# Gated linear attention and spectral filter on one core: token stage in 64-row parts, reversed key blocks, and products that may be issued in column tiles

## The chip, the cores and the metric

The kernel runs on one core of one Trainium2 chip. The metric is the device time of one launch in microseconds (us). Three runs of the kernel before the change took 241.71, 242.41 and 244.06 us, so its median is 242.41 us. Besides, one execution was profiled; durations and shares below are from that execution. The engines are named as in the profile: PE is the matrix engine (PEld its weight loads), DVE the vector engine, ACT the scalar engine, POOL the GpSimd engine, and SP the engine whose queue issues nearly all DMAs.

## The reference

The input x has 2048 tokens of 640 channels in bf16. Two branches read it, and a gate per token mixes them.

```python
x = A_x                                              # (1, 2048, 640)
g = sigmoid((x * gate_w).sum(-1, keepdims=True))
a = A(x)      # 32 heads of 20: per segment of 512 tokens causal softmax attention,
              # mixed with a read of a linear memory M, z that earlier segments filled
b = irfft2(rfft2(x) * (w_r + 1j * w_i))              # over tokens and channels
return g * a + (1 - g) * b
# inside A, for each of 4 segments s:
#   a_dot = softmax(q k^T / sqrt(20) + causal mask) v
#   a_mem = (phi(q) M) / (phi(q) z + 1e-6);  o = sig(beta) a_mem + (1 - sig(beta)) a_dot
#   M += phi(k)^T v;  z += sum phi(k)                ; finally o @ wo
```

## The kernel before, in words

**Attention branch.** For each segment s of 512 tokens, `project` makes q and k (products of 128 weight columns with 512 or twice 256 moving columns, `proj`, 195 operations), stores them to a scratch tensor and loads them back padded per head (`pad`). v is made per block of 128 tokens in two halves of 320 or 321 columns (`vproj`, 160 operations). The keys of the odd 128-token blocks stand in an order in which the two halves of 64 tokens are exchanged (`token_order`), and the v products of the odd blocks are issued as two tiles of 64 columns each so that their rows stand in that order too. `qk_unit` makes the logits of four heads in row tiles (80 units), ACT takes the exponential out of PSUM (92 instructions, line 1265), POOL zeroes what the causal mask forbids (`mask`, line 1286, 224 instructions), and `pv_flipped` (segments 0 to 2, four tiles of 32 columns) or `pv_group` (segment 3) multiplies with v. `mem_read` and `mem_update` serve the linear memory. `finish_tile` makes the output projection (`oproj`) and adds the filtered branch (`Fb`).

**Spectral branch (`fft`).** `fold` folds the channels on DVE and POOL (lines 902 and 907). `F1` (80 products of 128 columns) is the first factor of the token transform, with x split into 128 by 16. Then the token stage runs over 16 groups g. For each group: `D`, the channel transform, six products with 128 weight columns (three with 160 or 161 columns at each side, 321 in the middle), two evictions `ev_D`; `T`, the second token factor, four products of 321 columns (two outputs `ri`, each the sum of two); `W_mul`, two DVE instructions that multiply by the real and the imaginary filter at once (line 1441); `W_add`, two additions that make the complex product (line 1446, half of them on DVE, half on POOL); `Tb`, the inverse, six products of 256 columns, and two evictions `ev_Tb`. The filter rows come in 32 loads of 80 KB (`ld_W`), the tables of T and Tb in eight loads of 512 KB (`ld_tt`). Last come 16 inverse channel stages `Db` (96 products of 321 columns) and their sums `sum_Db` (line 1487).

**What sets the order.** Every operation is recorded once with what it reads and writes, and gets a number. A long tuple, `ORDER`, holds the sequence: entry v stands for operation v // 2 on its alternative v % 2. `schedule` runs through it with a cost table, gives each PSUM bank a place, and `emit` writes the instructions and the semaphore waits. Each engine works strictly in its order; SP's queue too.

**Array modes.** PE runs in one of four arrangements, which the code numbers: 0 is the whole array, 1 the row tiles of the logits, 2 four tiles of 32 columns, 4 two tiles of 64 columns. A matrix product has a fixed mode; only `oproj` may take 0 or 2. In the order of the kernel before the mode changes 232 times from one PE operation to the next, 160 of them into or out of the 80 logit units, and 72 between the other modes.

Lines that the steps of the prediction touch: 515 (products and weight loads), 513 (products issued as four tiles), 524 and 526 (evictions on ACT and DVE), 549 (DMA issues).

Of the kernel before, what the change touches and what calls it, by code (L numbers as in the profile page):

```python
# [20 lines left out]
VW = 22  # L21

# [22 lines left out]
class Op:  # L45
    __slots__ = ("id", "alts", "preds", "succs", "prio", "banks", "nbytes", "npred", "eng", "t0", "t1",
                 "stamp", "need_inc", "dyn", "first", "outside", "name", "dma", "key", "xfer", "lock", "mode", "emode", "hold", "width")


class Sched:  # L50
    HOP = 70.0
# [8 lines left out]
    def op(self, alts, r=(), w=(), prio=0.0, nbytes=0, name="", after=(), dma=False, xfer=0.0, lock=False, mode=0, hold=False, width=16):  # L60
# [24 lines left out]
        for b in w2:  # L85
            bb = b
            if isinstance(b, Bank):
                o.banks.append(b)
                b.ops.append(o)
                bb = b.buf  # L90
            dep(bb.w)
            for q in bb.r:
                dep(q)
# [10 lines left out]
        if name in ("gate_tab", "den_gate") and not o.banks:  # L104
# [4 lines left out]
    COST = {(0, 1): 94.0, (0, 2): 94.0, (1, 0): 110.0, (1, 2): 110.0, (2, 0): 110.0, (2, 1): 94.0,  # L109
            (0, 4): 105.0, (1, 4): 105.0, (2, 4): 105.0, (4, 0): 105.0, (4, 1): 105.0, (4, 2): 105.0}  # L110

    def schedule(self, pools, order, nsem=56):


        ops = self.ops
        queue = {e: [] for e in self.eng}
        for v in order:
            o = ops[v // 2]
            o.eng = list(o.alts)[v % 2]
            queue[o.eng].append(o)  # L120
        for o in ops:
            o.dyn, o.t1 = [], None
            o.first = [b for b in o.banks if b.ops[0] is o]
            for b in o.banks:
                b.left = len(b.ops)
        pe, held = queue["pe"], {}
        for i, o in enumerate(pe):
            o.emode = o.mode
            if o.mode < 0:
                modes = [held[id(b)] for b in o.banks if id(b) in held]  # L130
                if not modes and i and pe[i - 1].emode not in (1, 4):
                    modes = [pe[i - 1].emode]
                for q in pe[i + 1:] if not modes else ():
                    m = q.mode if q.mode >= 0 else held.get(id(q.banks[0]), -1)
                    if m >= 0:
                        modes = [0 if m == 1 else m]
                        break
                o.emode = (modes + [0])[0]
            if o.emode not in (1, 4):
                for b in o.banks:  # L140
                    held[id(b)] = o.emode
        pos = {e: 0 for e in self.eng}
        free = {e: 0.0 for e in self.eng}
        port = mode = 0
        level = {k: {q: 0.0 for q in v} for k, v in pools.items()}
        users = {}
        ring = [0.0] * 16
        sems = [[0.0, i, None] for i in range(nsem)]
        issued = []
        self.order = []  # L150

        def place(b, lev):
            best = None
            for pool in b.pools:
                v = lev[pool]
                for q in v:
                    run = [v.get(q + i) for i in range(b.n)]
                    if None not in run and (best is None or max(run) < best[0] - 1e-9):
                        best = (max(run), pool, q)
            return best  # L160

        def window():
            tot, i = 0, len(issued) - 1
            while i >= 0 and tot <= self.WINDOW:
                tot += issued[i].nbytes
                i -= 1
            return issued[i] if i >= 0 else None

        def head(e):
            if pos[e] == len(queue[e]):  # L170
                return None
            o = queue[e][pos[e]]
            t = free[e]
            for p in o.preds:
                if p.t1 is None:
                    return None
                if p.eng != "pe" or e != "pe":
                    t = max(t, p.t1 + self.HOP)
            if o.first:
                lev = {k: dict(v) for k, v in level.items()}  # L180
                for b in o.first:
                    got = place(b, lev)
                    if got is None:
                        return None
                    t = max(t, got[0])
                    for i in range(b.n):
                        lev[got[1]][got[2] + i] = None
            if o.dma:
                gate = window()
                if gate is not None:  # L190
                    t = max(t, gate.t1 + self.HOP)
            if e == "dve" and o.lock:
                t = max(t, free["pool"])
            elif e == "pool":
                t = max(t, port)
            return t

        while len(self.order) < len(order):
            best = None
            for e in self.eng:  # L200
                t = head(e)
                if t is not None and (best is None or t < best[0] - 1e-9):
                    best = (t, e)
            if best is None:
                raise RuntimeError("order cannot be kept: " + str([(e, queue[e][pos[e]].name, queue[e][pos[e]].id) for e in self.eng if pos[e] < len(queue[e])]))
            t, e = best
            o = queue[e][pos[e]]
            pos[e] += 1
            for b in o.first:
                _, b.pool, b.bank = place(b, level)  # L210
                for q in range(b.bank, b.bank + b.n):
                    level[b.pool][q] = None
                    o.dyn.extend(users.get(q, ()))
            o.t0 = t
            occ, lat = o.alts[e][1:]
            if e == "pe" and o.emode != mode:
                occ += self.COST[mode, o.emode]
                mode = o.emode
            free[e] = o.t1 = t + occ
            if e == "dve" and o.lock:  # L220
                port = t + occ
            if o.dma:
                if o.hold:
                    free[e] = max(free[e], max(ring) + 170.0)
                for q in range(o.width):
                    ring[q] = max(ring[q], free[e] + 1300.0) + o.xfer
                o.t1 = max(ring[:o.width])
                free[e] += 43.0
                gate = window()
                if gate is not None:  # L230
                    o.dyn.append(gate)
                issued.append(o)
                sems.sort(key=lambda q: (q[0], q[1]))
                sm = sems[0]
                if sm[2] is not None:
                    o.dyn.append(sm[2])
                sm[0], sm[2] = o.t1, o
                o.stamp = sm[1]
            o.t1 += lat
            self.order.append(o)  # L240
            for b in o.banks:
                b.left -= 1
                if b.left == 0:
                    for q in range(b.bank, b.bank + b.n):
                        users[q] = list(b.ops)
                        level[b.pool][q] = max(p.t1 for p in b.ops) + self.HOP
        self.makespan = max(o.t1 for o in ops)
# [215 lines left out]
class Kern:  # L463
# [342 lines left out]
    def record(self):  # L806
# [4 lines left out]
        for s in range(NSEG):  # L811
            self.project(s)
            if s > 0:
                self.mem_read(s)
# [794 lines left out]
```

## Time and profile before

| | before |
|---|---|
| runs | 241.71, 242.41, 244.06 us |
| span of the profiled execution | 239.9 us |
| between the span and the median of the runs | 2.5 us |
| PE busy | 225.7 us, 3837 products |
| ACT busy | 199.1 us |
| DVE busy | 195.9 us |
| POOL busy | 165.8 us |
| DMA | 42.11 MB, 176 GB/s on average |
| masks on POOL (line 1286) | 224 instructions, 121.3 us |
| W_add | 16 on DVE (5.5 us), 16 on POOL (11.7 us) |

The share of busy time of PE has to be read with care: a product's end is modelled, and a product of 256 columns is shown with 0.273 us although the next one starts after 0.11 us. What a product costs a full PE is the distance from start to start. In the view of stages, the columns are the window, its length, the busy time of each engine with the number of instructions, the granted clock, the busy share of the 16 DMA engines and what they moved. In the view of the timeline they are start, time from the first start to the last end of the merged row, engine, line and operation.

### The profile page before, as it was taken

To read this page: it belongs to the slowest core of one execution; us is meant where nothing else is said; L and a number is where in the kernel's file an instruction comes from. 1 tells how busy PE (TensorE), PEld (TensorE's weight loads), DVE (VectorE), ACT (ScalarE), POOL (GpSimd) and SP (SyncE) were. 2 spreads that over 40 slices of the span, in tenths; PEclk is the share of its full clock that TensorE was granted. 3 is DMA by queue.
4 is the path that set the end of the run, shared out by engine and by line. 5 is a ranking of instruction groups with operands and counts; after the bars stand their busy time and mean duration, and the time that the engine had idled before them with its cause. 6 is when DMAs were issued, how large, how long until landed. Compare 5 with 4: busy or idle time off the path is not lost.

```text
span 239.9 us, 9221 instructions
## 1 busy us (share of the span) xinstructions
PE 225.7 (94%) x3837; PEld 138.7 (58%) x3849; DVE 195.9 (82%) x481; ACT 199.1 (83%) x241; POOL 165.8 (69%) x297
## 2 busy tenths in 40 slices
PE   7899999999999999999989999899999998998994
PEld 2475567765456566455646555455544456665793
DVE  0479998889899996898999798997988887855563
ACT  2189688898899999999999979999999987896730
POOL 8514259457969956937974999875899867686820
PEclk9999999999999999999999999999999999999999
DMA  7999869984996795473788672364766698992223
GB/s 157 270 369 234 228 177 182 311 156 112 209 263 161 128 240 170 106 240 76 239 221 251 159 222 65 103 168 138 193 193 187 202 220 127 100 110 80 61 85 109
DMA packets 58924, 42.11 MB, mean 176 GB/s; under 512 B 30020, under 2 KB 55172, under 8 KB 58884
## 3 DMA queue, kind: packets, MB, share of 16 engines
q1 hardware_dynamic: 57844, 40.96, 70.2%
q8 instruction: 30, 0.49, 0.9%
q10 hardware_dynamic: 1040, 0.57, 0.8%
q14 instruction: 10, 0.08, 0.1%
HBM read 23.32 MB, written 12.30 MB: 148 GB/s over the span
## 4 chain that ended last, share of the span: by engine, by line
PE 57%; DVE 17%; ACT 15%; DMA 4%; issue 3%; SPq 2%; POOL 0%; DVEq 0%; ACTq 0%
PE psum L515 51%; ACT ex L1265 10%; PE psum L513 6%; DVE Pt L1441 3%; DMA out_dram<-ot 2%; DMA wk<-in_A_wk_dram 2%; SPq L547 2%; DVE xsb L907 2%; DVE xf L902 2%; ACT et L1073 1%; DVE va L1116 1%; DVE ub L526 1%; DVE phk L1086 1%; DVE q L526 1%; DVE phk L1085 1%
## 5 line engine op out<-in xcount | busy, mean ns | idle before, releaser
L1265 ACT ACTIVATE ex<-psum 128x2048 bf16<-128x2048 f32 (+4 forms) x92 | 138.7, 1507 | 12.6 <-PE psum L515 11.2
L1286 POOL TENSOR_SCALAR_AFFINE_SELECT ex<-ex 128x256 bf16<-128x256 bf16 (+2 forms) x224 | 121.3, 563 | 39.0 <-ACT ex L1265 35.6
L515 PE MATMUL psum<-xT,wk 128*128 128x256 bf16 (+1 forms) x280 | 34.0, 273 | 1.0 <-DMA wk<-in_A_wk_dram 0.8
L515 PE MATMUL psum<-qkp 20*64 20x64 bf16 (+5 forms) x1024 | 31.5, 266 | 3.4 <-ACT ex L1265 2.4
L515 PE MATMUL psum<-wv,xT 128*64 128x320 bf16 (+3 forms) x240 | 30.1, 303 | 0.4 <-DVE va L1116 0.3
L515 PE MATMUL psum<-xT,wq 128*128 128x512 bf16 (+1 forms) x123 | 27.1, 380 | 0.8 <-DMA xT<-in_A_x_dram 0.5
L1441 DVE TENSOR_TENSOR Pt<-psum,Wt 128x642 bf16<-128x642 f32 x32 | 25.6, 822 | 2.3 <-PE psum L515 1.9
L515 PEld LDWEIGHTS psum<-xT,wk 128*128 128x128 bf16 (+1 forms) x280 | 19.9, 97 | 7.5 <-DMA wk<-in_A_wk_dram 1.1
L515 PEld LDWEIGHTS psum<-qkp 20*64 20x64 bf16 (+1 forms) x1024 | 12.2, 100 | 20.4 <-ACT ex L1265 14.4
L513 PE MATMUL psum<-wo,oU 128*32 128x320 bf16 x480 | 21.9, 300 | 0.0
L907 POOL TENSOR_TENSOR xsb<-xf 128x320 bf16<-128x320 bf16 (+2 forms) x12 | 9.4, 787 | 16.6 <-DVE xsb L907 12.4
L515 PEld LDWEIGHTS psum<-wv,xT 128*64 128x64 bf16 (+1 forms) x240 | 14.9, 105 | 7.7 <-issue 2.6
L1116 DVE TENSOR_TENSOR va<-psum,ebx 128x320 bf16<-128x320 f32 x32 | 15.2, 483 | 4.4 <-ACT gate L1114 2.3
L515 PE MATMUL psum<-big,Ac 128*128 128x160 bf16 (+2 forms) x96 | 18.1, 258 | 0.7 <-DVE Pt L1441 0.3
L515 PE MATMUL psum<-big,Cp 128*128 128x321 bf16 (+1 forms) x96 | 18.1, 303 | 0.2 <-DVE G L1487 0.2
L515 PE MATMUL psum<-ex,va 128*32 128x512 bf16 (+4 forms) x480 | 17.3, 275 | 0.9 <-DVE Pt L1441 0.3
L1487 DVE TENSOR_TENSOR G<-eo,psum 128x320 bf16<-128x320 f32 x32 | 14.7, 482 | 3.5 <-PE psum L515 2.5
L526 DVE CAST ot<-psum 128x320 bf16<-128x320 f32 x21 | 10.0, 490 | 8.7 <-PE psum L513 5.3
L515 PE MATMUL psum<-tt,Yt 128*128 128x256 bf16 (+1 forms) x96 | 16.5, 275 | 0.3
L515 PEld LDWEIGHTS psum<-ex,va 128*32 128x32 bf16 x480 | 10.4, 96 | 9.9 <-POOL ex L1286 3.3
L1073 ACT ACTIVATE et<-qu 128x512 bf16<-128x512 bf16 x25 | 15.6, 629 | 0.2
L513 PEld LDWEIGHTS psum<-wo,oU 128*32 128x32 bf16 x480 | 12.0, 96 | 4.6 <-issue 1.2
(99 smaller groups left out, 391.1 us busy)
## 6 DMA issues: line engine op xcount, KB each, us to landing
qkp<-qk_scr SPq DMA_DIRECT2D x28, 160.0 KB
tt<-tab_tt SPq DMA_DIRECT2D x8, 512.0 KB, 3.9
qk_scr<-qu SPq DMA_DIRECT2D x12, 256.0 KB, 3.5
u_scr<-ub SPq DMA_DIRECT2D x12, 256.0 KB, 4.0
xsb<-in_A_x_dram SPq DMA_DIRECT2D x8, 320.0 KB, 6.4
oU<-u_scr SPq DMA_DIRECT2D x15, 128.0 KB, 3.1
out_dram<-ot SPq DMA_DIRECT2D x12, 160.0 KB
Wt<-in_B_w_r_dram SPq DMA_DIRECT2D x16, 80.2 KB, 3.4
```

Of the source, the lines that this page charges most:

```text
L513: h = e.matmul(dst, wt, r_, start=st, stop=sp_, **{**kw, "tile_position": (0, q), "skip_group_check": True})
L515: h = e.matmul(o_, l_, r_, start=st, stop=sp_, **kw)
L526: alts["dve"] = (lambda e: e.tensor_copy(dst(), src()), 67 + 1.04 * n, 68.0)
L547: return e.dma_start_transpose(d_, s_)
L902: self.either(lambda e, r=r, op=op: e.tensor_tensor(xf.ap(r * 642, [321, 2], [1, 320]), xs.ap(o, [D, 2], [1, 320]), xs.ap(o + 320, [D, 2], ...
L907: self.either(lambda e, dst=dst, src=src, d0=d0, n=n, op=op: e.tensor_tensor(xs.ap(o + dst, [D, 2], [1, n]), xf.ap(src + d0, [321, 2], [1, ...
L1073: self.one("act", lambda e: e.activation(et.ap(0, [1, L]), qsl(), ACT.Exp), L, [qb], [b("et", pi_)], late, name="phi_exp")
L1116: self.one("dve", lambda e: e.tensor_tensor(va.ap(i * H * VW + h0 * VW, [VW, nh], [1, DH]), self.ps(bank, 0, [DH, nh], [1, DH]), self.ebx. ...
L1265: self.one("act", lambda e, d=d, q=q: e.activation(self.ex.ap(*d), self.ps(bank, *q), ACT.Exp, scale=SC), n, [bank], [self.exb(s, 2 * pr + ...
L1286: self.one("pool", lambda e: e.affine_select(self.ex.ap(e0 + d0, [1280, 4], [1, n], np_=np_), self.ex.ap(e0 + s0, [1280, 4], [1, n], np_=np_),
L1441: self.one("dve", lambda e, ri=ri, Pt=Pt, Wt=Wt, wo_=wo_, bank=bank: e.tensor_tensor(Pt.ap(ri * 322, [644, 2], [1, KD]), self.ps(bank, 0, ...
L1487: self.one("dve", lambda e, q=q, n2=n2, bank=bank, eo=eo: e.tensor_tensor(self.G.ap(n2 * D + 639 * q, [1 - 2 * q, 320]), eo.ap(q, [1, 320] ...
```

## The change

1. **Token stage in 64-row parts.** Each group g is worked in two halves of 64 rows. `D` makes both kinds of a half (cosine and sine) side by side as two tiles of 64 columns into one bank: three pairs, one eviction. `T` then needs one product of 321 columns per half, because the two kinds stand together in its 128 contraction rows. `W_mul` stays, one per half. `W_add` is gone: its additions happen in `Tb`, whose table has the signs, with two products of 128 columns for each of three chunks of 107 rows (they were 128, 128 and 65); one eviction of 384 columns per half. `Db` reads chunks of 107.
2. **Filter rows.** A scratch tensor `w_scr` is filled by 20 DMAs from DRAM to DRAM (8 of 40 KB for the first two groups, then 4 of 281 KB and 8 of 140 KB), and each pair of groups then loads one block of 642 KB (8 `ld_W`; each row goes to two partitions). The tables of T and Tb shrink to 384 KB per load.
3. **Reversed key blocks.** The keys of odd blocks now stand in fully reversed order, read with step -1 by the k products. A copy `xR` of the odd blocks in reversed order (`xrev`, four instructions, two on ACT and two on POOL) makes the v products of odd blocks plain ones of 128 columns; the gate's column of these blocks is a product of its own with one column (40 of them). Eight of the 24 small gate exponentials go. The masks of a reversed block shrink, and those of the third kind are made for two groups at once where the buffers lie in ascending order: 191 masks instead of 224.
4. **Modes.** `proj`, `vproj`, `F1`, `T`, `Tb`, `Db`, `memrd`, `mupd` and `oproj` may be issued whole, as two tiles of 64 or as four tiles of 32 columns. The tuple `TILED` says for each (v // 8 is the operation, v % 8 its mode), `D` is 4 or 2.
5. **Order, banks, waits.** `ORDER` is new (2303 operations for 2328), the bank of each PSUM tile comes from a tuple `HOMES`, the cost table leaves the program, and a tuple `ENDED` sorts the waits of an instruction so that the one expected last is waited for last. An instruction no longer waits for an earlier one of its own engine when both only share a PSUM bank.

In the new order the mode changes 195 times: the same 160 at the logit units, 35 elsewhere.

```diff
+        tiled = {v // 8: v % 8 for v in tiled}
+        for o in pe:
+            o.emode = o.mode if o.mode >= 0 else tiled.get(o.id, 0 if o.mode == -1 else 4)
...
+    @staticmethod
+    def ordered(p, o):
+        return p.eng == o.eng and not p.dma and (p.eng == "pe" or p in o.preds and p.id not in o.hard)
...
-                if op.mode < 0 and op.emode == 2:
-                    m, pitch = l_.ap[1][1], l_.ap[1][0]
-                    for q in range(0, m, 32):
+                if op.mode < 0 and op.emode:
+                    m, pitch, w = l_.ap[1][1], l_.ap[1][0], 32 if op.emode == 2 else 64
+                    for q in range(0, m, w):
...
-        return [(0, 256, lambda: xT.ap(c * L, [256, 2], [1, P])), (256, 256, lambda: xT.ap(c * L + P + 64, [256, 2], [-64, 2], [1, 64]))]
+        return [(0, 256, lambda: xT.ap(c * L, [256, 2], [1, P])), (256, 256, lambda: xT.ap(c * L + 2 * P - 1, [256, 2], [-1, P]))]
...
+        rev = lambda: (xR.ap(0, [256, 5], [P, 2], [1, P]), xT.ap(2 * P - 1, [L, 5], [256, 2], [-1, P]))
+        self.Sc.op({"pool": (lambda e: e.tensor_copy(*rev()), 1340.0, 50.0), "act": (lambda e: e.activation(*rev(), ACT.Copy), 1130.0, 110.0)}, ...
...
+            if h0 and i % 2:
+                items.append(((lambda c=c: (self.ps(bank, 320, [1, 1]), xT.ap(c * L + i * P, [1, P]),
+                                            self.wv.ap(c * (D + 1) + D, [1, 1]), False, c == 4, {"skip_group_check": True})), 1))
...
-            for ri in range(2):
-                bank = Bank(1, "gen")
-                items = []
-                for q in range(2):
-                    def th(ri=ri, q=q, tt=tt, to=to, Bt=Bt, bank=bank):
-                        return (self.ps(bank, 0, [1, KD]), tt.ap(to + (2 * ri + q) * P, [1, P]), Bt.ap(q * 322, [1, KD]), q == 0, q == 1, {})
-                    items.append((th, KD))
...
-            for r, (a0, a1, op) in enumerate(((0, 3, ALU.subtract), (1, 2, ALU.add))):
-                fn = lambda e, ...: e.tensor_tensor(Yt.ap(r * 322, [1, KD]), Pt.ap(a0 * 322, [1, KD]), Pt.ap(a1 * 322, [1, KD]), op)
-                self.either(fn, KD, [Pb[0][r], Pb[1][1 - r]], [Yb[r]], prio2, ..., name="W_add")
...
+                def th(tt=tt, to=to, Bt=Bt, bank=bank):
+                    return (self.ps(bank, 0, [1, KD]), tt.ap(to, [1, P]), Bt.ap(0, [1, KD]), True, True, {})
+                self.mms([(th, KD)], [b("tt", ti), Bb, bank], [], prio2, name="T", mode=-1)
...
+                for c in range(3):
+                    items = []
+                    for x in range(2):
+                        def th(c=c, x=x, Pt=Pt, tt=tt, to=to, bank=bank):
+                            return (self.ps(bank, c * P, [1, P], np_=KN), Pt.ap(x * 322 + c * KN, [1, KN]), tt.ap(to + P + x * P, [1, P]), x == 0, x == 1, {})
...
+    def reorder_w(self, prio):
...
+                        for do, dst, so, src in moves:
+                            self.dma(lambda dst=dst, do=do, late=late: dap(self.Wd.ap(), late * 64 * pitch + do, *dst), lambda src=src, so=so, wd=wd: dap(wd, so, *src),
+                                     2 * dst[0][1] * dst[1][1] * dst[2][1], [], [b("Wd", late, n_)], prio + 2 * late, name="mv_W" + str(late))
```

## The prediction

> **What bounds the kernel now.** I read the page first, for the busy shares, then the stages, then the timeline of PE, because its busy time overstates what a product costs.
>
> ```profile
> PE 225.7 (94%) x3837; PEld 138.7 (58%) x3849; DVE 195.9 (82%) x481; ACT 199.1 (83%) x241; POOL 165.8 (69%) x297
> ```
> ```profile
> 0.00:15.00 15.00, 12.34 (x166) 6.65 (x167) 4.40 (x10) 4.38 (x6) 9.88 (x14) 1.00 0.95 248
> 15.00:50.00 35.00, 34.55 (x430) 23.10 (x429) 32.33 (x79) 30.56 (x50) 16.72 (x30) 1.00 1.00 234
> 50.00:80.00 30.00, 28.58 (x408) 16.77 (x411) 28.61 (x79) 27.81 (x31) 23.84 (x45) 1.00 0.74 174
> 80.00:120.00 40.00, 39.34 (x563) 23.05 (x564) 35.41 (x83) 38.52 (x46) 28.89 (x55) 1.00 0.67 176
> 120.00:160.00 40.00, 37.71 (x560) 21.41 (x561) 36.82 (x83) 37.21 (x38) 32.73 (x62) 1.00 0.61 165
> 160.00:190.00 30.00, 28.34 (x474) 15.73 (x475) 26.98 (x76) 28.01 (x35) 23.72 (x43) 1.00 0.65 179
> 190.00:215.00 25.00, 24.33 (x653) 15.78 (x645) 18.07 (x47) 21.39 (x26) 18.53 (x33) 1.00 0.95 156
> ```
> Columns of the stages after the length: PE, PEld, DVE, ACT, POOL, granted clock, DMA share, GB/s. From 15 to 190 us PE is busy to 96%; from 50 on ACT follows with 93 to 96% and DVE with 89 to 95%. PE is the bound, with little slack beside it. DMA is full up to 50 us.
>
> ```profile
> 85.95 0.45 PE L515 MATMUL psum<-Bt,tt 128*128 128x321 bf16 x2
> 86.24 0.38 PE L515 MATMUL psum<-xT,wk 128*128 128x256 bf16 x2
> 86.46 0.44 PE L515 MATMUL psum<-Bt,tt 128*128 128x321 bf16 x2
> 86.83 0.73 PE L515 MATMUL psum<-ex,va 128*32 128x512 bf16 x20
> 87.49 0.87 PE L515 MATMUL psum<-wv,xT 128*64 128x320 bf16 x10
> 88.29 0.39 PE L515 MATMUL psum<-xT,wk 128*128 128x256 bf16 x2
> 88.61 0.40 PE L515 MATMUL psum<-qkp 20*128 20x320 bf16 x8
> 88.94 1.26 PE L515 MATMUL psum<-xT,wk 128*128 128x256 bf16 x10
> ```
> These rows give three prices. **Columns:** the last row's ten products of 256 columns take 1.26 us to the end of the last; one lasts 0.273 in the list by shape, so nine starts take 0.99, 0.110 us each, or 0.42 ns per column and 3 ns. A product of 321 columns thus costs 0.137, of 128 columns 0.056. **Tiles:** the twenty products of the probability step are 1280 columns in five pieces, four tiles at a time. **A switch of the mode** is what is left of the distance between two starts: 86.46 to 86.83 is 0.37 for two products of 0.137, left 0.10; 86.83 to 87.49 is 0.66 for 1280 columns (0.54), left 0.12; 87.49 to 88.29 is 0.80 for five pairs of 0.137, left 0.12; 88.29 to 88.61 leaves 0.10; 88.61 to 88.94 is 0.33 for 512 columns, left 0.12. I take 0.11 us. There are 232 switches: 25 us in which PE is shown busy.
>
> **The change, part by part, on PE.**
> - T: 64 products become 32. 32 x 0.137 = **-4.4 us**.
> - D: six products of 161, 321, 160 columns per group become two times three pairs of the same lengths: 0.
> - Tb: 96 x 0.110 = 10.6 become 192 x 0.056 = 10.8: **+0.2**. Db, proj, F1 keep their columns.
> - v of odd blocks: 80 pairs at 0.137 become 80 products at 0.137, and 40 one-column products are new. Products of 21 columns are 25 ns apart (in the attention of segment 3 the timeline has 28 of them over 0.85 us, the last one lasting 0.17); 15 of the 40 are issued whole, the rest in tiles: 40 x 0.025 = 1.0 at most, 0 at least; **+0.6**.
> - Switches: 232 to 195 by the two order lists, 37 x 0.11 = **-4.1** (0.10 and 0.12: -3.7 and -4.4).
> - Tiled products: two or four products and weight loads where there was one, by the list some 1800 more of each. The twenty products above span 0.51 us from the first start to the last (0.73 less the last one's 0.22, the mean of its shape) for 1152 columns, 0.48: sixteen starts cost 0.03, the loads of a 64-column piece included. So four loads fit beside 64 columns (0.027), and a piece of 128 has twice the time. Two loads of 64 columns, by the same 128 columns of weights, fit too: **0**, at most 0.5 for the 102 pairs of Tb that just fit.
> - The k products of odd blocks read with step -1. No PE row does. One end is 0 (the same columns). The other is DVE's reversed fold: 318 elements take 0.465 where 322 take 0.326, 43% more; on 100 products of 0.107 that is 4.6. A gain is excluded, as the present ones already stream at a column per 0.42 ns. I take **0**, since the shorter fold row and the forward row W_add (321 elements, 0.365) lie together.
>
> The short tiled products are where this could fail: the new list tiles 93 of the 96 Tb operations (186 groups of 128 columns) and 16 of F1 (32 groups). A weight load is shown with 0.096 us for 32 columns and 0.097 for 128; did one load set the pace of a group instead of its columns (0.056), 218 x 0.041 = 8.9 us would come on top. The Trainium skill speaks for that: its page "TensorEngine Tiling (Array Packing)", Restrictions, says that column tiling turns off the fast weight load. The 64-column piece above, with four loads in 0.03 us, speaks against it, so the rule is a rival and no term.
>
> Sum on PE: -4.4 + 0.2 + 0.6 - 4.1 = **-7.7 us**.
>
> **The other engines.** ACT: 7 fewer evictions of D (0.538 each), 5 fewer of Tb and shorter (5.8 to 3.4), 3 of Db, 8 gate exponentials of 0.165, 2 of oT3, against two reversed copies of 1280 elements (1.3 each, from 0.602 for 512 and 0.435 for 320) and two F1 evictions: about -8 us. It falls as PE does and covers nothing new. POOL: masks. One of 128x256 is 0.478, of 128x512 0.691, of 64x512 0.670. Now 128 x 0.478, 64 x 0.670, 32 x 0.691 = 124; after, 32 of the first kind at 0.478 and 32 at 0.691, 64 of the second at 0.478, 33 merged at 0.69 and 30 at 0.478 = 105. W_add goes (11.7), copies come (2 x 1.4 to 2.8; its 128x640 row is 1.40), and a few operations move in: -24 us. POOL bounds nothing. **DVE** is the one that gains nothing: W_add -5.5, but 7 evictions of D (+3.6), 25 of Tb at 0.55 for 20 (+2.9), some others: +2 us, from 195.9 to 198. In the shorter middle it rises from 91% (127.8 of 140 us between 50 and 190) to about 95%.
>
> **Queues.** SP issues 229 instead of 232. The filter moves are 2.63 MB from DRAM to DRAM, the loads grow from 2.63 to 5.26, the tables shrink from 4.19 to 3.15: 4.2 MB more on 42.1. The first eight moves (0.33 MB) stand among the first x loads. The other twelve come between the 32 and 54 us marks of pure column time, so about 38 to 66 us. The second block load waits for all twelve, and behind it in SP's queue stand pads and two transposes of the keys. At 234 GB/s 2.3 MB are 9.8 us of DMA; the stage from 50 to 80 has 26% of 30 us, 7.8, free, and the rest lies before the first use. I cost it at 0; if that cover is gone it is a rival below.
>
> **Stalls.** PE is idle for 6.7 us between 50 and 215 us (length less busy, row by row), mostly for exponentials. POOL and ACT loads that fall, waits sorted by their end, and dropped waits on the own engine can only shorten them or leave room for others: so between 0 and -5; I take **-1**, as ACT stays nearly full. Start and end are left alone.
>
> Span 239.9 - 7.7 - 1.0 = 231.2. The median of the runs is 2.5 us over the span, so **233.7 us**.
>
> **Rivals.**
> - *DVE holds the middle.* With 95% asked of it, products wait for its evictions and half of the gain is lost: 238 to 240. For it: its 28.61 of 30 us at 50 to 80. Against: few waits of PE name it (the longest total is 3.8 us of weight loads behind Pt).
> - *The stalls shrink by all of their 5 us*, and the switch costs 0.12: 229. For it: most idle time stands behind ACT, which is relieved.
> - *The moves delay the loads: slower than before.* Place: 15 to 65 us, where the DMA engines are full. Price: 2.63 MB of moves and the first block's 0.66 at 234 GB/s are 14 us; all of it in front of the pads that the next logits need gives 233.7 + 14 = 248. It decides once 8.7 us of it reach the path; with 8 it is no change, 242. Against it: the chain of this stage is PE and DVE, and one wait of DVE for x (1.1 us) is all that DMA costs there.
> - *The loads of tiled products set the pace:* 8.9 us, 242.6, no change. The row of a single load speaks for it, the twenty tiled products against. The Trainium skill's tiling rule above is on its side.
> - *The reversed read costs:* by the fold row 4.6 us, 238.3; if it halves the rate, 100 x 0.107, 244.4. No row of PE speaks either way; the two DVE rows disagree.
> - *It doesn't do what it says:* the list might keep its switches. Its entries say 195, so I give this nothing.
>
> **Chances.** Forecast, 231 to 238: 0.50. Deep, under 231: 0.17. DVE, or a reversed read at 4.6 us, 238 to 240: 0.11. Within 1% (2.4 us, about what a measurement tells from no change): 0.11, of it 0.04 a part of the DMA delay, 0.04 the tiled loads and 0.03 the read at half rate. Slower: 0.11, DMA 0.09, loads and read together (253) 0.02. So faster 0.78, same 0.11, slower 0.11. The range 227 to 243 leaves out the slower cases, the upper part of the no-change cases (0.05) and the deepest 0.04.
>
> **What would show it.** T's products: 32 groups, half the columns. PE's rows with 128*64 and 128*32 shapes for proj, v, Tb; groups of four tiles of 128 columns 0.06 apart or not. k products 0.110 apart, or about 0.2 if reversal costs. W_add absent, DVE at about 198 us, ACT at 191, POOL at 142. The DMA row of 15 to 80 us, and whether W_mul or the logits wait for Wt or qkp there. The prediction is wrong if the order leaves more idle time on PE than now, or if ACT and DVE cannot follow.

## The result and the profile after

The changed kernel takes **328.86 us** (median of four runs, 327.15 to 329.68), the kernel before 242.06 us in the runs beside it: ratio **1.3546** (95% interval 1.3481 to 1.3611). The forecast was 233.7 us, with a range of 227 to 243. Runs that lie more than 1.5% above the fastest of the same kernel are left out wherever times are compared below (column "compared" of the table).

The page of the changed kernel, busy times and the chain that ended last (by engine), and behind it the same chain of the kernel before:

```profile
PE 233.6 (71%) x5706; PEld 154.3 (47%) x5706; DVE 197.2 (60%) x478; ACT 193.3 (59%) x217; POOL 135.3 (41%) x255
...
PE 33%; DMA 32%; SPq 11%; issue 10%; ACT 8%; DVE 4%; POOL 1%; DVEq 0%; ACTq 0%
```
```profile
PE 57%; DVE 17%; ACT 15%; DMA 4%; issue 3%; SPq 2%; POOL 0%; DVEq 0%; ACTq 0%
```

DVE, ACT and POOL do about the work that was forecast for them (DVE 197.2 against 198, ACT 193.3 against 191, POOL 135.3 against 142). The span, 326.9 us, is long because they stand still: transfers, which were 4% of the chain before, are 32% of it, and "issue", time in which an engine waits for nothing that the profile shows, is 10% where it was 3%.

The stages, with columns as in the prediction:

```profile
15.00:50.00 35.00, 30.70 (x484) 20.24 (x472) 28.69 (x75) 29.16 (x45) 12.77 (x20) 1.00 1.01 240
50.00:80.00 30.00, 15.14 (x361) 10.81 (x363) 10.54 (x27) 11.16 (x14) 8.25 (x20) 0.77 0.76 101
80.00:120.00 40.00, 24.74 (x714) 15.94 (x708) 21.79 (x56) 24.38 (x26) 15.46 (x32) 0.83 0.83 145
120.00:160.00 40.00, 25.68 (x578) 16.81 (x578) 21.61 (x45) 20.59 (x23) 11.31 (x23) 0.79 1.11 104
215.00:240.00 25.00, 11.69 (x288) 6.21 (x276) 8.91 (x16) 11.78 (x11) 6.42 (x13) 0.80 0.38 119
...
270.00:300.00 30.00, 29.86 (x855) 20.10 (x851) 24.80 (x66) 24.16 (x29) 20.93 (x37) 1.00 0.72 142
```

From 50 to 240 us all four engines have idle time together (PE 24 to 53% of each stage), so none of them is the bound; and the DMA engines, which should then be the bound, move 101 to 145 GB/s where they moved 240 before 50 us. The last filter load ends at 242 us, and from 270 us on PE is full again.

The longest waits (engine, for whom, us in total, times, longest), and pieces of the chain (start, us, what):

```profile
DVE Pt L1529 <- DMA Wt<-w_scr: 29.5, 3, 11.4
...
PE psum L449 <- DVE Pt L1529: 20.9, 3, 11.3
...
PE psum L449 <- issue: 16.2, 2, 14.5
```
```profile
54.02 14.48 issue
...
106.12 19.01 DMA Wt<-w_scr
...
134.32 16.07 DMA qk_scr<-qu
...
160.50 10.90 issue
...
204.08 17.97 DMA qk_scr<-qu
222.80 18.96 DMA Wt<-w_scr
```

Three kinds of waits share the loss: for the filter block itself (19 us for 642 KB), for stores of q and k that have nothing to do with the filter (16 and 18 us, for 256 KB that landed in 3.5 us before), and for nothing that is shown.

What happens in such a stretch, from the stages and from the timeline of SP's queue and PE (start, us, engine, line; in brackets the idle time before):

```profile
52.00:62.00 10.00, 2.02 (x55) 1.36 (x46) 3.08 (x10) 2.05 (x2) 2.34 (x5) 0.85 0.13 52
```
```profile
47.64 16.90 SPq L483 DMA_TRANSPOSE xT<-in_A_x_dram  x1
...
68.50 1.28 PE L449 MATMUL psum<-wv,xT 128*64 128x321 bf16 x8 [14.48 <-issue]
```

The DMA share of 0.13 is two engines of sixteen, and 52 GB/s is what they move. (The share counts a packet in the window in which it starts.) The packets that start between 52 and 62 us are 102 of 5136 bytes, each a row of the filter block (about 0.2 us each, two at a time), and no others at all. Behind this load a transpose keeps SP's queue for 16.90 us, and PE stands still. The eight loads are 1024 such packets, 128 each: 12.8 us for a load if nothing else runs.

The other engines are not simply free meanwhile. Sixteen packets of 256 bytes, which by their time belong to the transpose, start at 51.8 us and end only at 64.2: 12.4 us each, where no packet of the kernel before takes over 2.7. Four of the eight loads have a transpose beside them and 16 to 22 such packets hanging; in the middle of three of these loads (from 2 us after the first packet to 1 us before the last) at most 12 other packets start. The other four loads have none, and in their middle 537 to 916 other packets start, 0.7 to 1.0 MB. So the full stop comes with load and transpose together, while a load alone lets others move and still makes them late: the store of q and k at 204.08 us takes 17.97 us beside a load without a transpose. No run here has the loads without the transposes, so how the loss divides between the two stays open.

### The profile page after: what moved, and what is told of

It reads as the page before. It is cut to its first block, busy times and chain, and to the rows that moved or that the text cites. A ratio compares the mean times of both kernels' runs of the same rounds, so it can differ in the third digit from the quotient of the medians.

```text
span 326.9 us, 12884 instructions
## 1 busy us (share of the span) xinstructions
PE 233.6 (71%) x5706; PEld 154.3 (47%) x5706; DVE 197.2 (60%) x478; ACT 193.3 (59%) x217; POOL 135.3 (41%) x255
## 2 busy tenths in 40 slices
DMA packets 59851, 46.56 MB, mean 142 GB/s; under 512 B 29844, under 2 KB 57108, under 8 KB 59796
## 4 chain that ended last, share of the span: by engine, by line
PE 33%; DMA 32%; SPq 11%; issue 10%; ACT 8%; DVE 4%; POOL 1%; DVEq 0%; ACTq 0%
PE psum L451 17%; PE psum L449 17%; DMA qk_scr<-qu 15%; DMA Wt<-w_scr 12%; SPq L483 7%; ACT ex L1353 6%; SPq L485 4%; DMA w_scr<-in_B_w_r_dram 3%; DMA xsb<-in_A_x_dram 2%; DMA wv<-in_gate_w_dram 1%; DVE qu L462 1%; POOL xsb L983 1%; DVE ot L462 1%; ACT qu L460 1%; ACT ub L460 1%
## 5 line engine op out<-in xcount | busy, mean ns | idle before, releaser
L1353 ACT ACTIVATE ex<-psum 128x2048 bf16<-128x2048 f32 (+4 forms) x92 | 137.2, 1505 | 30.7 <-PE psum L451 28.2
L1379 POOL TENSOR_SCALAR_AFFINE_SELECT ex<-ex 128x256 bf16<-128x256 bf16 (+3 forms) x191 | 93.6, 512 | 118.6 <-ACT ex L1353 114.3
L449 PE MATMUL psum<-Bt,tt 128*32 128x321 bf16 (+1 forms) x94 | 10.8, 350 | 32.7 <-DVE Pt L1529 20.8
L449 PE MATMUL psum<-wv,xT 128*32 128x321 bf16 (+5 forms) x240 | 16.3, 277 | 14.5 <-issue 14.5
L449 PE MATMUL psum<-xT,wk 128*32 128x256 bf16 (+1 forms) x500 | 25.6, 292 | 1.2 <-ACT qkp L460 1.0
L449 PE MATMUL psum<-xT,wq 128*32 128x512 bf16 (+1 forms) x230 | 23.7, 397 | 0.4 <-DVE qu L462 0.2
L1158 ACT ACTIVATE et<-qu 128x512 bf16<-128x512 bf16 x25 | 15.3, 625 | 12.2 <-DVE phq L1171 11.7
L462 DVE CAST qu<-psum 128x512 bf16<-128x512 f32 x16 | 11.0, 686 | 16.4 <-DMA qk_scr<-qu 12.7
L449 PEld LDWEIGHTS psum<-xT,wk 128*32 128x32 bf16 (+1 forms) x500 | 18.2, 108 | 4.1 <-ACT qkp L460 1.2
L460 ACT ACTIVATE qu<-psum 128x512 bf16<-128x512 f32 x14 | 8.2, 598 | 20.1 <-PE psum L449 12.3
L449 PE MATMUL psum<-tt,Pt 128*32 128x128 bf16 (+3 forms) x540 | 18.6, 234 | 0.2
L449 PE MATMUL psum<-big,Ac 128*32 128x321 bf16 (+5 forms) x264 | 17.8, 279 | 0.0
```

Source lines behind the costliest of these rows:

```text
L449: h = e.matmul(dst, wt, r_, start=st, stop=sp_, **{**kw, "tile_position": (0, q + o_.offset // 4096), "skip_group_check": True})
L460: alts["act"] = (lambda e: e.activation(dst(), src(), ACT.Copy), 65 + 0.833 * n, 110.0)
L462: alts["dve"] = (lambda e: e.tensor_copy(dst(), src()), 67 + 1.04 * n, 68.0)
L1158: self.one("act", lambda e: e.activation(et.ap(0, [1, L]), qsl(), ACT.Exp), L, [qb], [b("et", pi_)], late, name="phi_exp")
L1353: self.one("act", lambda e, d=d, q=q: e.activation(self.ex.ap(*d), self.ps(bank, *q), ACT.Exp, scale=SC), n, [bank], [self.exb(s, 2 * pr + ...
L1379: self.one("pool", lambda e: e.affine_select(self.ex.ap(e0 + d0, [1280, n4], [1, n], np_=np_), self.ex.ap(e0 + s0, [1280, n4], [1, n], np_ ...
```

## The experiments

**Theory A**: the load `ld_W` runs on two DMA engines of sixteen, because its source is written as (twice the same, 64 rows, 5136 bytes), with an outermost dimension of 2, and while it does, whatever has a share on these two engines waits. The rivals were the moves from DRAM to DRAM with the doubled volume, and the repeated read of one row. A kernel given without a range was timed once.

### w16: the same load on all engines

```diff
-  self.dma(lambda Wt=Wt: Wt.ap(0, [1, 8 * KD]), lambda g=g: dap(self.Wd.ap(), g // 2 * 64 * 8 * KD, [0, 2], [8 * KD, 64], [1, 8 * KD]), ...
+  return [e.dma_start(Wt.ap(0, [1, 8 * KD], p0=64 * h, np_=64),
+                      dap(self.Wd.ap(), g // 2 * 64 * 8 * KD, [8 * KD, 64], [1, 8 * KD])) for h in range(2)]
```

> The new kernel with one edit: each block load of the filter, one DMA that reads 64 rows twice (outermost source dimension 2, stride 0) into 128 partitions, becomes two DMAs of 64 rows into 64 partitions each, on the same semaphore. Same bytes, same order, eight more issues of 0.57 us on SP. In the profile of the new kernel the 1024 packets of these loads (128 per load) come at about 50 per 5 us and take 0.198 us each, which is two at a time: the theory is that a load whose outermost dimension is 2 is spread over two DMA engines, lasts 13 us on them, and holds up every other transfer that has a share on those two. Theory: all 85 us of loss go away and the time is that of the blind forecast, 231 to 238 us. Rival 1, the 2.63 MB of moves and the doubled load volume delay the path: still 245 or more, with waits for w_scr and Wt. Rival 2, the loss is in the order or in the tiled products: above 300.

Measured: 267.44 us (four runs, 262.76 to 272.58; the kernel before beside it 243.58); compared, 263.5. The same bytes land in the same partitions and the kernel ends 65.4 us earlier, so the shape of one access pattern is worth 8.2 us per load. But theory A had forecast 231 to 238 and missed: the kernel is still 20 us slower than the one before, in the range of rival 1 (245 or more), though without its waits for the filter (2.9 us in all). Theory A is right and not the whole of it.

### w2_perm and w4_perm: two and four engines without a repeated read

```diff
-  dap(self.Wd.ap(), g // 2 * 64 * 8 * KD, [8 * KD, 64], [1, 8 * KD])
+  dap(self.Wd.ap(), g // 2 * 64 * 8 * KD, [8 * KD, 2], [2 * 8 * KD, 32], [1, 8 * KD])     # w2_perm
+  dap(self.Wd.ap(), g // 2 * 64 * 8 * KD, [8 * KD, 4], [4 * 8 * KD, 16], [1, 8 * KD])     # w4_perm
```

> As w16 (two DMAs of 64 rows), but each reads its 64 rows as 2 times 32 (row i + 2j to partition 32i + j), so that the outermost source dimension is again 2, without a repeated read. The rows of the filter then stand in other partitions, which changes the result and no amount of work. Theory of the two engines: back to 320 to 335 us, Wt landing 13 us or more after its issue. Rival, that reading the same rows twice was slow, or that one DMA instead of two was: 231 to 245.

> As w2_perm with 4 times 16 rows (row i + 4j to partition 16i + j; filter rows permuted in the same sense). Theory: four DMA engines, 6.4 us of transfer per load, so the time lies between: 242 to 290 us, the packets of 5136 bytes four at a time. Rival, a matter of yes or no (outermost dimension under 16): the same as w2_perm.

Measured: 341.32 and 290.73 us, 6.3 and 0.7 us above the two expected ranges and far from the rivals. With w16 that is a row: outermost dimension 2, 4 and 64 give 341, 291 and 264 us for the same bytes in the same number of DMAs. The number of engines is the cause, not the row read twice. The Trainium skill states the rule on its page "DMA: Bandwidth & Descriptors", section "Why a DMA increments its semaphore by 16 and not by 1": a transfer is dealt out to the largest number of engines, up to 16, that divides the slowest dimension of both patterns. The traces agree: two rows in flight at a time in the changed kernel and w2_perm, four in w4_perm.

### dummy2: a load on two engines that nobody waits for

```diff
+  e.dma_start(dap(self.Wx.ap(), g // 2 * 128 * 8 * KD, [8 * KD, 128], [1, 2560]),
+              dap(self.Wd.ap(), g // 2 * 64 * 8 * KD, [0, 2], [8 * KD, 64], [1, 2560])).then_inc(self.xsem, 16)
   return [e.dma_start(Wt.ap(0, [1, 8 * KD], p0=64 * h, np_=64), ...
```

> w16, and in front of each block load one more DMA from DRAM to DRAM, 128 rows of 5120 bytes with the outermost dimension 2, whose result nobody reads and nobody waits for before the end of the kernel. It tells which of two ways the loss takes. Theory A, the occupied engines hold up all other transfers (stores and reloads of q and k, tables): most of the loss comes back, 290 us or more, with the real Wt loads late too, since they queue on the same engines. Theory B, only the wait of the filter product for its own block matters: within 10 us of w16.

Measured: 352.31 us, 88.8 more than w16, for eight copies whose data nothing reads. So the loss comes back without a load on two engines that anybody waits for. This run alone doesn't rule out a late filter: the real loads stand behind the copies, and DVE waits 44.4 us for them. The next two runs take it further.

### b_two and b_sixteen: the same copies in the kernel before

```diff
+                def extra(e, g=g):                      # ahead of the first filter load of a pair of groups
+                    o = g // 2 * 128 * 8 * KD
+                    e.dma_start(dap(self.Wx.ap(), o, [8 * KD, 128], [1, 8 * KD]),
+                                dap(self.wr_d, 0, [0, 2], [32 * KD, 64], [1, 8 * KD])).then_inc(self.xsem, 16)      # b_two
+                    for h in range(2):                                                                              # b_sixteen
+                        e.dma_start(dap(self.Wx.ap(), o + h * 64 * 8 * KD, [8 * KD, 64], [1, 8 * KD]),
+                                    dap(self.wr_d, 0, [32 * KD, 64], [1, 8 * KD])).then_inc(self.xsem, 16)
```

> The kernel before the change, complete and with its own result, plus eight copies of 657 KB from DRAM to DRAM that nothing needs, each put into SP's queue ahead of the first filter load of a pair of groups; only the end of the kernel waits for them. The source is written as (twice the same, 64 rows, 5136 bytes), as in the changed kernel's filter load, so each copy goes through two DMA engines. Theory A (a copy that sits on two engines holds up whatever has a share on these two, the other transfers and the fetch of instructions): the same copies cost the kernel w16 85 us, 10.6 each, so 243 + 60 to 85 = 303 to 328; PE gaps behind instruction packets, 0.6 us in the kernel before, above 10. Rival B (the changed kernel is sensitive by its new order; an old, fuller order rides over copies that it doesn't wait for): 243 to 255.

> As b_two with the same 5.26 MB, each copy written as two of 64 rows, which go through sixteen engines. Theory A: only the traffic counts; thin and w16 show 6 us for 2.6 MB of copies and their place, so 243 + 3 to 14 = 246 to 257. Rival B (it is the volume, not the two engines): as b_two.

Measured: **336.90** and **254.79** us, the kernel before 244.28 beside them: 11.6 us for each copy (657,408 bytes, 642 KB in the profile's units) on two engines, 1.3 us for each on sixteen. b_two lies 9 us above theory A's range, b_sixteen within it. A stretch of b_two, and some of its waits:

```profile
74.00:82.00 8.00, 4.69 (x74) 2.34 (x74) 3.82 (x13) 4.28 (x5) 4.84 (x10) 1.00 0.13 53
```
```profile
PE psum L515 <- DMA qkp<-qk_scr: 21.8, 2, 11.2
...
DVE dnr L1217 <- DMA dnc<-u_scr: 19.4, 2, 10.6
```

Again 0.13 and 53 GB/s, in a kernel without any part of the change, and its waits for data are mostly for other data than the filter, for which DVE waits once, 11.1 us; rival B is out. Here too four of the eight copies have 16 to 19 packets of 256 bytes hanging beside them. One detail of theory A failed: no gap of PE in b_two ends behind an instruction packet; its waits are for data.

### What is left: whole, thin, whole_thin

In w16 the waits of PE (by line) look like this; before the change no wait of PE for "issue" was longer than 0.2 us, 0.3 us in all:

```profile
PE psum L450 <- issue: 10.7, 10, 2.9
PE psum L450 <- DVE Pt L1534: 2.8, 2, 2.6
...
PE psum L452 <- issue: 1.8, 2, 1.0
```

The profile lists the DMA queues by kind (packets, MB, share of 16 engines). One is named "instruction"; its packets are 16,384 bytes. First the row of the kernel before, then the changed kernel's, then that of whole, a kernel told of next:

```profile
q8 instruction: 30, 0.49, 0.9%
```
```profile
q8 instruction: 45, 0.74, 1.0%
```
```profile
q8 instruction: 28, 0.46, 0.8%
```

The kernel before has 30 for its 3,849 products, the changed one 45 for 5,706. That is a packet for each 256 instructions of PE, where a product and its weight load are two. The Trainium skill, page "Runtime: NRT & Kernel Launch", section "Instruction fetch mechanics", gives the same size (16 KiB, 256 instructions) and calls the cost mostly hidden. In these traces it isn't hidden. In w16 PE has 25 gaps over 0.3 us (neither a product nor a weight load runs), 26.5 us in all, and 16 of them with 15.2 us end 0.6 to 2.0 us after such a packet has landed; in the longest two the packet landed 1.22 and 1.29 us before PE went on. In the kernel before it is 0.6 of 7.6 us, no more than chance gives. The place of the gaps says more than their time: 12 of the 16, with 12.8 us, begin after 1,472 products and weight loads or after a whole multiple of 256 more (1,728, 2,496, 4,800 and so on), where a packet is used up. In the changed kernel PE stops at the same places of its program, at other times: its gap from 54.02 to 68.50 us is the one at 1,728, that from 160.68 to 171.40 the one at 4,800 (its trace has one record more ahead of them). Hence **theory F**: tiles double or quadruple the instructions, and where transfers crowd the engines the fetch falls behind.

```diff
-    TILED = (
-        908, 916, 924, ...
+    TILED = (                                      # whole, whole_thin
     )
...
+                            dst, src = [[1, KD]], [[1, KD]]                                     # thin, whole_thin
...
-  dap(self.Wd.ap(), g // 2 * 64 * 8 * KD, [8 * KD, 64], [1, 8 * KD])
+  dap(self.wr_d, g // 2 * 4 * KD, [16 * KD, 64], [1, 8 * KD])                                   # thin, whole_thin
```

> As w16 (the filter load as two transfers of 64 rows), and the list of products issued as tiles is empty: every whole-array product goes out whole, 3,611 matmuls where w16 has 5,706; order, transfers and result are unchanged. In w16 (267.4 us) PE stands still for 26.5 us in gaps over 0.3 us, and 15.2 us of these end 0.6 to 1.6 us after a 16 KB packet of the instruction queue has landed; w16 has 45 such packets, the kernel before 30 and 0.6 us of such gaps. Theory F (PE waits for its own instructions: more of them, behind transfers): some 29 packets, gaps behind a packet under 3 us, granted clock back from 0.969 to 0.99 or more, so 267.4 - 12 to 15 - 5 to 8 (clock); but the array's shape now changes 310 times in the order where it changed 195 times, 115 x 0.11 = 12.6 us on PE: 257 us (246 to 264). Theory M (late data by the moves and the doubled filter volume, not instructions): nothing saved, the changes of shape added: 280 us (272 to 285), packets 29 but gaps as long as in w16. Theory O (the new order alone): 267 to 280, with the gaps behind DVE, ACT and data rather than behind packets.

> As w16, but each of the 20 moves of filter rows from DRAM to DRAM copies 642 bytes only, so that the 2.63 MB are not moved, and the filter loads (same size, same partitions, same waits) read rows of the first filter input instead, so the numbers that come out are for another filter. Instructions, order and queues are those of w16. Theory F (PE waits for its instructions because fetches stand behind transfers): still 45 instruction packets, but less ahead of them between 15 and 80 us; gaps behind packets 15.2 -> 6 to 10 us, above all those at 47 and 55 us; time 252 to 262. Theory M (the moves delay data): time 242 to 252, all gaps gone but those under 0.5 us. Theory O (order): 264 to 268.

> Both: only whole-array products and moves of 642 bytes (another filter, as in thin). Theory F: 29 packets and few transfers ahead of them, gaps behind packets under 1 us, clock 1.0; what is left against the kernel before is 310 - 232 = 78 more changes of shape, 8.6 us on PE, and 4.4 us less of products: 240 to 250. Theory M: the price of the changes of shape above thin: 250 to 262. Theory O: 264 or more.

| | us, median (range) | compared | ratio to before | PE changes shape | instruction packets | gaps of PE over 0.3 us | of these behind a packet |
|---|---|---|---|---|---|---|---|
| before | 242.06 to 244.24 | 242.06 to 243.93 | | 232 | 30 | 7.6 | 0.6 |
| after | 328.86 (327.15 to 329.68) | 328.86 | 1.355 | 195 | 45 | 87.6 | 29.4 |
| w16 | 267.44 (262.76 to 272.58) | 263.50 | | 195 | 45 | 26.5 | 15.2 |
| thin | 261.38 (255.68 to 265.22) | 257.24 | 1.058 (1.048 to 1.069) | 195 | 45 | 23.0 | 12.0 |
| whole | 252.90 (249.53 to 254.10) | 252.70 | 1.036 (1.027 to 1.045) | 310 | 28 | 14.2 | 0.7 |
| whole_thin | 246.32 (244.53 to 248.19) | 246.32 | 1.016 (1.006 to 1.025) | 310 | 28 | 8.8 | 0.0 |
| few | 247.76 (245.60 to 250.75) | 246.40 | 1.015 (1.003 to 1.027) | 226 | 32 | 15.7 | 1.5 |
| few_thin | 246.94 (246.07 to 247.79) | 246.94 | 1.014 (1.006 to 1.022) | 226 | 32 | 12.2 | 0.4 |
| whole_k2 | 324.11 | 324.11 | | 310 | 28 | 68.2 | 0.4 |

The first row gives the medians of the kernel before in the series that were run beside the others; each ratio is to its own series.

whole fell in theory F's range (246 to 264) and far from the other two (267 and more): with the tiles gone the kernel is **10.8 us faster although its array changes shape 115 times more**, and the gaps behind packets are gone. thin (252 to 262 by theory F) took 6.3 us off, three of them from gaps behind packets, which stayed at 12.0 where 6 to 10 were expected: fewer transfers help the fetch little, fewer instructions help it entirely. whole_thin gives the moves' price without the fetch, 6.4 us, and lies in theory F's range too (240 to 250).

### few and few_thin: as many tiles as the fetch bears

The list of tiles was chosen anew, so that the array seldom changes shape for few extra products: 4,068 products.

```diff
-        908, 916, 924, ...                          # 667 entries
+        ...                                         # 227 entries
```

> As w16 and whole, with another list of products issued as tiles: chosen so that the array's shape changes seldom for few extra matmuls (groups of one bank kept together): 4,068 matmuls (whole 3,611, w16 5,706), 226 changes of shape (whole 310, w16 195). Order, transfers and result unchanged. Theory F (tiles cost only where the fetch of instructions falls behind; with about 32 packets it does not): 252.9 - 84 x 0.11 = 243.7, plus 0 to 3: 245 (240 to 249), gaps behind packets under 3 us. Rival P (each extra matmul costs, wherever it stands: w16 is 14.5 us over whole although it saves 115 x 0.11 = 12.6 us, so 27 us for 2,095 matmuls, 0.013 each): 243.7 + 457 x 0.013 = 249.6 (248 to 252).

> few, with moves of 642 bytes and the filter loads reading rows of the first filter input (numbers of another filter, as in thin). whole_thin lay 6.6 us under whole. Theory F: 246.3 - 84 x 0.11 = 237.1 (234 to 241), which would be faster than the kernel before, as the terms of the prediction other than the transfers have it (233.7, with 195 changes of shape: 233.7 + 31 x 0.11 = 237.1). Rival P: 237.1 + 5.9 = 243. If it is 243 or more, the remaining terms of the prediction (the T products, the stalls) failed as well.

few came in at 247.76, compared 246.40: in theory F's range, above its value of 245 and 1.6 us under rival P's 248 to 252, while its runs reach from 245.60 to 250.75, so its time hardly parts the two; its gaps behind packets (1.5 us of 15.7) speak for F. It is the best kernel here that computes the whole, 6.3 us under whole, and by its ratio still 1.5% over the kernel before (0.3 to 2.7%). few_thin is a **miss**: 246.94 against 237.1 by either the prediction's remaining terms or theory F, above rival P's 243 too. Taking away the moves gave nothing any more, and the fetch had nothing left to give. So more of the prediction was wrong than its transfers; the section on the prediction says where the time stands.

### whole_k2: only the tiles undone

```diff
-    TILED = (
-        908, 916, 924, ...
+    TILED = (
     )
```

> The changed kernel with nothing but its list of tiled products emptied: filter loads as one transfer each again (two engines), 3,611 matmuls, 310 changes of shape. Theory F: the 29 us of gaps behind instruction packets that the changed kernel has shrink with 28 packets instead of 45, yet a load lasts 13 to 19 us and two blocks of instructions are used up in that time, so not to nothing: 10 to 20 us; the waits for filter rows and q/k stay (about 55 us); +12.6 for the changes of shape: 328.9 - 15 + 12.6 = 326 (312 to 335). If tiles alone were the cause, it would come down to whole's 253.

Measured: 324.11 us, as expected in sum, but not in its parts: gaps behind packets are 0.4 us, not 10 to 20. With 28 packets the fetch keeps up even beside loads on two engines. That the time (of one run) still fell by 4.8 us only shows that the waits of the changed kernel overlap: what one of them gave back, waits for data took (68.2 us of gaps remain).

## Why the prediction was wrong, step by step

- **Queues: the failed step.** I put the filter loads and moves at 0, from their bytes at 234 GB/s, on the stage's free DMA time. The bytes were right (46.56 MB for 42.11, 4.4 more where 4.2 was forecast). Three things were missing in the price. The loads had two of sixteen engines, 52 GB/s, and held up the others' transfers, above all where a transpose stood beside them: 65.4 us (after to w16). The tiles' instructions are DMA traffic too, and late: 10.8 us net (w16 to whole). The moves cost 6.3 to 6.4 us (w16 to thin, whole to whole_thin). From 328.9 these lead to 263.5, 252.7 and 246.3 us.
- **What stays** between whole_thin and the kernel before, 246.32 against 243.07 beside it, is 3.3 us. 78 more changes of shape at about 0.1 us less the 4.3 us of T make 3.5. By the two traces (the split is told under Switches) it is 4.3 less for T, 5.8 more in short losses, 0.07 for each of the 78 changes, and 2.0 more in long waits: the sum fits, the price of a change was somewhat high.
- **T, -4.4: right.** By the form of its products T has 8.56 us of columns before (64 of 321 at 2.4 columns per ns) and 4.28 after; the columns of the other operations are equal in both traces, but for 12 q products (2.6 us) whose records are missing before.
- **Reversed read, 0: right.** Ten k products, whole, half of them reversed, in the timeline of whole; the row of the kernel before, quoted in the prediction, has the same 1.26 us:

```profile
100.95 1.26 PE L452 MATMUL psum<-xT,wk 128*128 128x256 bf16 x10
```

- **Tiled products, 0 (at most 0.5): right for the loads, by an estimate too low in sum.** The rival had a weight load set the pace, 0.097 us for each group of Tb. In the timeline of the changed kernel six groups of Tb as pairs take 0.34 us to the next row's start, 0.057 each, as priced, and six untiled ones in whole take the same 0.34 (102.05 to 102.39). The Trainium skill's rule that column tiling turns off the fast weight load ("TensorEngine Tiling (Array Packing)", Restrictions) doesn't show in this time. The rows:

```profile
133.29 0.50 PE L449 MATMUL psum<-tt,Pt 128*64 128x128 bf16 x12
133.63 0.44 PE L449 MATMUL psum<-wv,xT 128*64 128x320 bf16 x4
```

- **Switches, -4.1: not seen.** I took the line of PE from the first product to the last and subtracted the columns. Of what is lost in each stretch between two changes of shape, the first 0.5 us count as one part and the rest as the other. The first part is 48.5 us in the kernel before with 232 changes, 48.7 in w16 with 195, 48.9 in few_thin with 226 and 54.3 in whole_thin with 310. (Records of 12, 1, 8 and 14 products are missing, so these values may be up to 2.6, 0.2, 1.3 and 2.5 us too high.) From few_thin to whole_thin 84 changes more are 4 to 5 us more, so a change costs something, by an estimate 0.05 to 0.08 us. From few_thin to w16 31 changes go, some 2 us, and 1,638 products come; that the sum stays about equal puts 1 to 2 ns on each extra product. Both are estimates from these four numbers, not tested by themselves, and w16 had a lower mean clock as well (0.969 against 0.986). The two terms together brought about nothing in place of -4.1.
- **Stalls, -1: wrong sign.** The second part, beyond 0.5 us, is 9.0 us before, 30.7 in w16, 11.0 in whole_thin and still 15.8 in few_thin, where neither the moves nor the fetch is left. That is how few_thin missed: against whole_thin its 84 fewer changes gave 4 to 5 us, not 9.2, and its long waits took 4.8 more. The longest of them behind the start, 2.3 us at 75 us, is for the second filter block:

```profile
70.39 6.50 DMA Wt<-in_B_w_r_dram
```

  After it, and once more at about 208 us, the granted clock was 0.50 for 3.4 us; whole_thin had a mean clock of 0.999. Whether the new order or the larger block (642 KB where the kernel before loads 80 KB at a time) makes the wait is not shown. I had read the relief of ACT and POOL as fewer stalls; that was argued from busy times, which came out about as forecast and decided nothing.
- **ACT and POOL, sums.** The parts that the prediction lists for ACT come to -6.2, not -8; measured is -5.8. The masks before are 126.2 by its prices, not 124 (121.3 on the page), and after 93.6 where it had 105 (a mask of 128x256 took 0.435, not the 0.478 it was priced at). ACT and POOL were not the bound, so this decided nothing.
- **The rival "the moves delay the loads"** had the right side, with 0.09, and a place where it began (15 to 65 us; the loss goes on to 242), but the wrong mechanism and a sixth of the price. "DVE holds the middle" played no part: DVE waited.

## What to carry to other kernels

Price a transfer by the engines it runs on before its bytes: look at the outermost dimension of both of its patterns, and in the trace for stretches in which the DMA share is a small multiple of 1/16 while every engine idles. A transfer on few engines can cost nearly its whole length to everyone, even if nobody waits for it: 11.6 us of the 13 to 14 that a copy lasted, against 1.3 for the same 642 KB on sixteen. Look also at what stands right behind it in the queue; here the worst stops had a transpose there. And count the instructions that a finer tiling makes: they come by DMA, 16 KB at a time, and an engine that needs a packet each 6 us (45 in the 261 us of w16) stands still when the fetch has to queue.

## What the runs showed of the hardware that I had not expected

- While a transfer on two engines ran, sixteen 256-byte packets of the transpose behind it hung for 12.4 us, and no packet of any other transfer started from 52 to 62 us. SP could not even finish issuing the transpose: it took 16.90 us, in w16 at the same place 6.91, in the kernel before 4.36.
- PE's instructions pass through a DMA queue, and PE stops where a packet is used up: in w16 it starts 256 products and weight loads, one packet's worth, between its gaps at 49.96 and 55.11 us. Counted from these places, in the kernel before each packet starts when 148 to 283 of the instructions already fetched are left, so PE lives on about one packet ahead; in w16 it is 0 at the two long gaps. After a late packet PE went on 1.2 to 1.5 us after its end (w16: 48.74 to 49.96, 56.68 to 57.97; after: 67.02 to 68.50).
- Standing still costs twice. In w16 PE is idle from 55.11 to 57.97 us, and then, though it is full, has a granted clock of 0.50 for six us (last three columns: clock, DMA share, GB/s):

```profile
58.00:60.00 2.00, 2.00 (x24) 0.78 (x24) 0.00 (x0) 0.69 (x2) 0.17 (x1) 0.50 0.44 141
60.00:62.00 2.00, 2.00 (x60) 1.73 (x56) 0.72 (x2) 1.61 (x1) 0.00 (x0) 0.50 0.04 8
62.00:64.00 2.00, 2.00 (x42) 1.38 (x34) 0.57 (x2) 0.43 (x2) 1.45 (x4) 0.50 0.00 0
```

  In the changed kernel the mean clock is 0.877, and its PE is shown busier (233.6 us) than before (225.7) with fewer columns to do.
